# A gated bilinear unit beside an FFT filter: new dependences, priorities and load estimates in a list-scheduled kernel

## The chip, the cores and the metric

The kernel runs on one core of one Trainium2 chip. A core has TensorE (PE, matrix products into PSUM), VectorE (DVE), ScalarE (ACT), GpSimd (POOL), SyncE (SP, which here issues DMAs) and 16 DMA engines. The metric is the device time in microseconds of one execution; for each kernel the median of several is given.

## The reference

The input x has 2048 rows of 640 bf16 values. Each row is normalized, and two things are computed from the normalized rows: a two-dimensional real FFT that is multiplied by a complex weight and transformed back, and a bilinear gated unit. Both are added to x.

```python
def _layernorm(x, axis=-1, eps=1e-5):
    m = jnp.mean(x, axis=axis, keepdims=True)
    v = jnp.var(x, axis=axis, keepdims=True)
    return (x - m) / jnp.sqrt(v + eps)
...
    X = rfft2(x.astype(jnp.float32)); X = X * (w_r + 1j * w_i); y = irfft2(X, s=(S, D)).astype(jnp.bfloat16)
...
    g = jnp.einsum("bsd,df->bsf", x, w_gate)
    u = jnp.einsum("bsd,df->bsf", x, w_up)
    return jnp.einsum("bsf,fd->bsd", g * u, w_down)
...
    xn = _layernorm(x, axis=-1)
    return x + _A_ref(xn, A_w_r, A_w_i) + _B_ref(xn, B_w_gate, B_w_up, B_w_down)
```

(The transforms' lambdas are written out shorter here; S is 2048, D 640, F 1536.)

## The kernel before

**Tiles.** x lies in SBUF as 16 "rows" b = 0 to 15, each a tile of 128 partitions by 640 values (2048 / 16 tokens). It comes in six loads (`_X_LOADS`): rows 0, 1, 2 and 3 each alone, then 4 to 7, then 8 to 15. The gate and up weights come in five pairs of loads (`_GW_LOADS`): of the 12 column blocks f of 128, blocks 0-1, 2-3, 4-5, 6-7, and 8-11. All these go through SP's queue, in one order, except the first up load and a small table, which ACT issues.

**A planner decides the order.** Nothing runs in the order in which the source makes it. `_build` makes tasks (`T`, `dma`), each with an engine or a choice of two, a modelled duration, a priority, and dependences that follow from what it reads and writes (or are added by hand in `deps`). `_Sched.plan` is a list scheduler: for each engine it takes the ready task of best priority, lets another go first that would end within that task's start plus a slack (`slack`, per engine), and thereby fixes one static order per engine, as well as which engine makes a copy and which PSUM bank a product gets. Loads are modelled by bytes over `dma_bw` plus `_DMA_LAT`. The modelled times do nothing on the chip; there each engine walks through its list in that order, and waits at each task for the semaphores of its dependences. So an instruction that waits holds all that stand behind it on its engine.

**Normalizing a row** (lines 758 to 821). For rows 0 to 5: two statistics instructions on DVE (`bn`, L778), their merge (`ag`, L786), adding epsilon (`ve`, L799), a square root on ACT (`sd`, L803), a reciprocal on DVE (`rs`, L807), and two passes over the row: subtract the mean (`sub`, L814) and scale (`mul`, L821, tasks `muls[b]`). For rows 6 to 15 the statistics are made on ACT: `sm` (L763, the mean) and `sq` (L769, the squares), each an ACTIVATE that accumulates, followed by a read of the accumulator, and merged on DVE (`mb`, L791). From row 4 on, two rows share `ve`, `sd` and `rs`.

**Transposing.** Rows 0 to 3 are transposed by PE: `T0_b`, five products with the identity (L839) into PSUM, copied to the tile XT by ACT and DVE in two parts for rows 0 and 1, in one part for rows 2 and 3 (L715 on ACT, L716 on DVE). Rows 4 to 15 go by a transposing DMA that SP issues when the row is scaled (`xt`, L827).

**Gate and up products.** `GU_f_b` multiplies XT of a chunk of rows by the weight block f; the chunks are rows 0; 1; 2-3; 4-7; 8-11; 12-15. For the first two chunks one task holds ten matmuls of 128 columns, for rows 2-3 ten of 256 (both L984), from row 4 on gate and up are two tasks of five matmuls with 512 columns (L964). Such a task holds one PSUM bank, and at most two may be held by this class (cap "glu"); a copy to SBUF frees it (`eG`, nearly always ACT, L715: 128 x 256 for the first chunks, 128 x 512 after them), and DVE multiplies the two (`H`, L1001 and L1000) into the tile HT.

**The transform.** Steps `S1` to `S5` on DVE (L878 to L912) combine pairs of normalized rows, `R` (L925, five matmuls for each row, copied out by `eR`) begins the transform along the rows, `D` (L1029), `C` (L1050 to L1053), the product with the complex weight (`WM`, L1065 to L1068) and `IA` (L1112, L1113) follow, then `I` (L1141) and `V1` to `V5` on DVE.

**The end.** For each row a and half, `ACC` (L1216) sums twelve matmuls of 320 columns from HT and the down weights, `IV` (L1224) adds the last product of the transform into the same bank, DVE adds x (`FIN`, L1231), and SP stores the result.

**At the start.** PE runs 48 matmuls on zeros (L743) and then, while it has nothing to do, pairs of filler products (L732, L733).

The units of gate and up products are put in order by when their rows (`c_at`) and weights (`w_at`) are due:

```python
        w_at = [6.0 + opts.get("w_rate", 2.2) * min(ft // 2, 4) for ft in range(12)]
        c_at = [6.3 + opts.get("c_rate", 2.2) * (b0 + nb - 1) for b0, nb in _CHUNKS]
```

and by hand row 1's statistics are held back, the first until row 0 is scaled and the second until its transposed copy is made:

```python
                    if b == 1:
                        bns[0].deps.add(muls[0])
                        bns[1].deps.add(e0_first)
```

Of the kernel before, what the change touches and what calls it, by code (L numbers as in the profile page):

```python
# [12 lines left out]
_TAIL = {"pe": 165.0, "act": 90.0, "dve": 90.0, "pool": 100.0, "sp": 0.0}  # L13
_DMA_BW = 350.0
_DMA_LEAD = 500.0
_DMA_LAT = 1000.0
_START = 680.0
_DMA_ISSUE = 500.0

# [52 lines left out]
class _Sched(object):  # L72
    def __init__(self):
        self.tasks = []
        self.bufs = []
        self.caps = {}
        self.window = 250.0
        self.affinity = 600.0
        self.dma_bw = _DMA_BW
        self.slack = {"pe": 1000.0, "act": 300.0, "dve": 400.0, "pool": 100.0, "sp": 0.0}  # L80
        self.order = None
        self.makespan = 0.0

    def buf(self, name, off, size):
# [69 lines left out]
    def plan(self, nbanks=8, filler_deadline=0.0):  # L154
# [56 lines left out]
        while nsch < ntot:  # L211
# [41 lines left out]
            for e_ in by_eng:  # L253
                lst = by_eng[e_]
                hb = None
                for c in lst:
                    k = (c[3].prio, c[0], c[3].tid)
                    if hb is None or k < hb[0]:
                        hb = (k, c)
                hc = hb[1]  # L260
                slack = self.slack.get(e_, 100.0)
                ch_ = None
                for c in lst:
                    if c is hc or c[1] <= hc[0] + slack:
                        k = (c[0], c[3].prio, c[3].tid)
                        if ch_ is None or k < ch_[0]:
                            ch_ = (k, c)
                c = ch_[1]
                k = (c[0], c[3].prio, c[3].tid)
                if pick is None or k < pick[0]:  # L270
                    pick = (k, c)
            est, fin, e, t, unit_choice = pick[1]
# [26 lines left out]
            if unit_choice is not None:  # L299
                k0 = unit_choice[1]  # L300
                nb = 2 if unit_choice[0] == "pair" else 1
# [247 lines left out]
def _build(nc, A_x, A_w_r, A_w_i, B_w_gate, B_w_up, B_w_down, out, opts=None):  # L549
# [3 lines left out]
    with es:  # L553
# [153 lines left out]
        def dma(name, dst, src, nbytes, writes, prio, semkey=None, reads=(), after=(), q="sp"):  # L707
            def em(c):
                return c.e.dma_start(dst, src)  # L709
            return T(name, q, _DMA_ISSUE, em, reads=reads, writes=writes, prio=prio, nbytes=nbytes,  # L710
                     semkey=semkey, after=after)
# [40 lines left out]


        for gi, (b0, nb) in enumerate(_X_LOADS):
            dma("ld_x%d" % gi, v_x[:, b0:b0 + nb, :], xv[:, b0:b0 + nb, :], 128 * nb * 1280,
                [(b_x, ("s", b0, b0 + nb))], prio=(0.0, 0.003, 0.02, 0.03, 0.042, 0.06)[gi])
        muls = {}
        for gi, (b0, nb) in enumerate(_LN_GROUPS):
            pbase = 1.0 + 0.05 * gi if gi < 4 else opts.get("ln_prio", 5.9) + 0.05 * (gi - opts.get("ln_lead", 2))
            for b in range(b0, b0 + nb):  # L760
                if b >= opts.get("act_stats", 6):
                    def em_sm(c, b=b):
                        return c.e.activation(v_jk, v_x[:, b, :], _ACTF.Copy, scale=1.0 / _D,  # L763
                                              accum_out=v_m32[:, b:b + 1])
                    T("sm%d" % b, "act", _d_act(640) + 93, em_sm, reads=[(b_x, ("s", b, b + 1))],
                      writes=[(b_m32, ("b", b, b + 1)), (b_jk, None)], prio=pbase)

                    def em_sq(c, b=b):
                        return c.e.activation(v_jk, v_x[:, b, :], _ACTF.Square, scale=-1.0, bias=v_m32[:, b:b + 1],  # L769
                                              accum_out=v_ss[:, b:b + 1])  # L770
                    T("sq%d" % b, "act", _d_act(640) + 186, em_sq,
                      reads=[(b_x, ("s", b, b + 1)), (b_m32, ("b", b, b + 1))],
                      writes=[(b_ss, ("b", b, b + 1)), (b_jk, None)], prio=pbase)
                else:
                    bns = []
                    for i in range(2):
                        def em_bn(c, b=b, i=i):
                            return c.e.bn_stats(v_st[:, b, 6 * i:6 * i + 6], v_x[:, b, 320 * i:320 * i + 320])  # L778
                        bns.append(T("bn%d_%d" % (b, i), "dve", 420.0, em_bn, reads=[(b_x, ("s", b, b + 1))],
                                     writes=[(b_st, ("b", 2 * b + i, 2 * b + i + 1))], prio=pbase))  # L780
                    if b == 1:
                        bns[0].deps.add(muls[0])
                        bns[1].deps.add(e0_first)

                    def em_ag(c, b=b):
                        return c.e.bn_aggr(v_mv[:, b, :], v_st[:, b, :])  # L786
                    T("ag%d" % b, "dve", 176.0, em_ag, reads=[(b_st, ("b", 2 * b, 2 * b + 2))],
                      writes=[(b_mv, ("b", b, b + 1))], prio=pbase)
# [151 lines left out]
        for i, (f0, nf) in enumerate(_GW_LOADS):  # L940
            for w_ in range(2):
                dma("ld_gw%d_%d" % (f0, w_), v_gw[:, w_, :, f0:f0 + nf, :].rearrange("p j r f -> p j (r f)"),
                    gvs[w_][:, :, f0 * 128:(f0 + nf) * 128], 5 * 128 * nf * 256,
                    [(b_gw, ("s", w_ * _NGW + f0, w_ * _NGW + f0 + nf))], prio=(0.004, 0.012, 0.022, 0.032, 0.05)[i] + 0.001 * w_,
                    q="act" if w_ and i < 1 else "sp")
        w_at = [6.0 + opts.get("w_rate", 2.2) * min(ft // 2, 4) for ft in range(12)]
        c_at = [6.3 + opts.get("c_rate", 2.2) * (b0 + nb - 1) for b0, nb in _CHUNKS]
        units = sorted((max(c_at[ci], w_at[ft | 1]), ci, ft) for ci in range(len(_CHUNKS))
                       for ft in range(0, 12, 1 if _CHUNKS[ci][1] == 4 else 2))
        for ui, (at_, ci, ft0) in enumerate(units):  # L950
# [177 lines left out]
            dma("ld_wd%d" % f0, v_wd[:, f0:f1], wdv[:, f0:f1], 128 * (f1 - f0) * 1280,  # L1128
                [(b_wd, ("e", 640 * f0, 640 * f1))], prio=18.0 if f0 < 7 else 9.6, after=[muls[opts.get("w_after", 15)]])
        for a in range(16):  # L1130
            pa = 19.0 + opts.get("i_rate", 0.05) * a
            pc = 41.0 + 0.05 * a
            r2 = a % 2

# [68 lines left out]
        for a in range(16):  # L1203
            pc = opts.get("acc_prio", 41.0) + 0.05 * a
            xs = a % 4
            dma("ld_xr%d" % a, v_xr[:, xs, :], xv[:, a, :], 128 * 1280, [(b_xr, ("r", xs, xs + 1))],
                prio=pc, semkey=("xr", xs))
            for hf in range(2):
                ro = 2 * (a % 2) + hf
                sl3 = slice(hf * 320, (hf + 1) * 320)  # L1210

                def em_ag2(c, a=a, sl3=sl3):
                    bk = bank_of(c.t)
                    ins = None
                    for ft in _FT_ORDER:
                        ins = c.e.matmul(ps[:, bk, 0:320], v_ht[:, ft, a * 128:(a + 1) * 128], v_wd[:, ft, sl3],  # L1216
                                         start=(ft == 7), stop=False)
                    return ins
                ag2 = T("ACC_%d_%d" % (a, hf), "pe", 12 * _d_mm(320), em_ag2,
                        reads=[(b_ht, ("col", a, a + 1)), (b_wd, None)],  # L1220
                        prio=pc + 0.01 + 0.001 * hf, bank="single", cls="acc")

                def em_iv(c, ag2=ag2, a=a, sl3=sl3):
                    return c.e.matmul(ps[:, bank_of(ag2), 0:320], v_sm[:, 2, :], v_v[:, a, sl3], start=False,  # L1224
                                      stop=True)
                iv = T("IV_%d_%d" % (a, hf), "pe", _d_mm(320), em_iv,
                       reads=[(b_v, ("a", a, a + 1)), (b_sm, ("t", 1, 3))], prio=opts.get("iv_prio", 19.0) + 0.05 * a + 0.01 + 0.001 * hf, after=[ag2])

                def em_f1(c, ag2=ag2, a=a, xs=xs, sl3=sl3):
                    bk = bank_of(ag2)  # L1230
                    return c.e.tensor_tensor(v_out[:, a % 2, sl3], ps[:, bk, 0:320], v_xr[:, xs, sl3], _OP.add)  # L1231
                f1 = T("FIN_%d_%d" % (a, hf), "dve", _d_dve_psum(320), em_f1,
                       reads=[(b_xr, ("r", xs, xs + 1))], writes=[(b_out, ("r", ro, ro + 1))], prio=opts.get("fin_prio", 41.0) + 0.05 * a - 0.001,
                       frees=ag2, after=[iv])
                dma("st_out%d_%d" % (a, hf), ov[:, a, sl3], v_out[:, a % 2, sl3], 128 * 640, [], prio=pc - 0.003,
                    reads=[(b_out, ("r", ro, ro + 1))], semkey=("out", ro))

        sch.window = 100.0
        sch.slack["act"] = opts.get("slack_act", 500.0)
        sch.slack["dve"] = opts.get("slack_dve", 600.0)  # L1240
        sch.slack["pe"] = opts.get("slack_pe", 1500.0)
        sch.affinity = opts.get("affinity", 300.0)
        sch.dma_bw = float(opts.get("dma_bw", 310.0))
        sch.plan(8, filler_deadline=opts.get("fill_deadline", 7600.0))
        sch.compute_waits()
        if opts.get("report") is not None:
# [75 lines left out]
```

## Time and profile before

| | |
|---|---|
| median of 4 executions | 208.67 us (207.82, 208.33, 209.01, 209.74) |
| the profiled execution | 207.82 us, its span in the profile 206.0 us |
| granted TensorE clock | 1.000 |
| HBM read, written | 16.82 MB, 2.62 MB |

The span is what the profile sees, from the first to the last instruction; the execution's time is 1.82 us longer. The page's coarse view of the span, 40 slices of 5.15 us, each digit the busy share in tenths:

```profile
PE   7988999999999999999999999999999999999994
DVE  4698999999999999949997996917999999999941
ACT  2377989999876666577999899878422022000000
DMA  6999990603118843001323353225033133224211
```

TensorE's row is full but for the first 20 us and the end; the DMA engines are full from about 5 to 30 us, while the weights, the rows and the tables come in. "PE" in the views is the matmuls, "PEld" the weight loads that overlap them. In the timelines an instruction's entry has its start, its duration, engine, line and operation, and in brackets how long its engine was idle before it and what ended that.

### The profile page before, as it was taken

What the parts mean: (1) busy time and instruction counts of PE and PEld (TensorE: products, weight loads), DVE (VectorE), ACT (ScalarE), POOL (GpSimd) and SP (SyncE); (2) the same over time, 40 slices, a digit from 0 to 9 for tenths busy, and PEclk for the clock granted to TensorE, in tenths of its full rate; (3) what the DMA queues carried; (4) which work ended last, traced back from release to release, by engine and by line L of the source; (5) the groups of instructions that cost most, each with busy time, mean ns of one, the idle gap of its engine ahead of it and who ended that gap; (6) DMA issues with size and microseconds to landing.
All of it is one profiled execution on the core that took longest, in us unless ns stands there. A gap on an engine that the chain in (4) does not pass through costs nothing.

```text
span 206.0 us, 4482 instructions
## 1 busy us (share of the span) xinstructions
PE 200.7 (97%) x1682; PEld 136.5 (66%) x1682; DVE 178.2 (87%) x507; ACT 121.3 (59%) x282; POOL 21.8 (11%) x36
## 2 busy tenths in 40 slices
PE   7988999999999999999999999999999999999994
PEld 7888899645455455465766666656777777777772
DVE  4698999999999999949997996917999999999941
ACT  2377989999876666577999899878422022000000
POOL 0000000000000000003655365310000000000000
PEclk9999999999999999999999999999999999999999
DMA  6999990603118843001323353225033133224211
GB/s 182 300 342 378 393 198 7 61 6 64 32 33 73 251 111 122 3 0 24 68 58 61 62 119 67 67 65 158 3 98 93 44 104 121 86 67 112 83 48 48
DMA packets 30596, 21.69 MB, mean 105 GB/s; under 512 B 10480, under 2 KB 29552, under 8 KB 30448
## 3 DMA queue, kind: packets, MB, share of 16 engines
q1 hardware_dynamic: 29776, 21.06, 41.2%
q10 hardware_dynamic: 800, 0.36, 0.6%
q8 instruction: 13, 0.21, 0.5%
q14 instruction: 7, 0.06, 0.1%
HBM read 16.82 MB, written 2.62 MB: 94 GB/s over the span
## 4 chain that ended last, share of the span: by engine, by line
PE 89%; SPq 4%; DMA 4%; DVE 1%; issue 0%; DVEq 0%
PE ps L964 38%; PE ps L1216 25%; PE ps L984 9%; SPq L709 4%; DMA arena<-in_A_x_dram 4%; PE ps L1029 2%; PE ps L1113 2%; PE ps L925 2%; PE ps L1141 2%; PE ps L1112 2%; PE ps L1224 2%; PE ps L1050 1%; PE ps L1053 1%; PE ps L1052 1%; PE ps L1051 1%; DVE arena L778 1%
## 5 line engine op out<-in xcount | busy, mean ns | idle before, releaser
L715 ACT ACTIVATE arena<-ps 128x512 bf16<-128x512 f32 (+6 forms) x182 | 96.7, 567 | 48.7 <-PE ps L1141 22.6
L964 PE MATMUL ps<-arena 128*128 128x512 bf16 x360 | 82.6, 379 | 0.0
L964 PEld LDWEIGHTS ps<-arena 128*128 128x128 bf16 x360 | 33.8, 98 | 36.5 <-ACT arena L715 1.4
L1216 PE MATMUL ps<-arena 128*128 128x320 bf16 x384 | 56.5, 299 | 0.0
L1216 PEld LDWEIGHTS ps<-arena 128*128 128x128 bf16 x384 | 37.3, 98 | 14.1
L984 PE MATMUL ps<-arena 128*128 128x128 bf16 (+1 forms) x360 | 27.9, 237 | 1.3 <-DVE arena L799 0.6
L984 PEld LDWEIGHTS ps<-arena 128*128 128x128 bf16 x360 | 25.2, 98 | 3.4 <-ACT arena L715 1.4
L1065 DVE TENSOR_TENSOR arena<-ps,arena 128x256 f32<-128x256 f32 x64 | 22.6, 417 | 1.4 <-PE ps L1053 1.4
L1000 DVE TENSOR_TENSOR arena<-arena 128x512 bf16<-128x512 bf16 x36 | 15.4, 427 | 8.8 <-ACT arena L715 8.7
L1088 POOL TENSOR_TENSOR arena<-arena 128x256 bf16<-128x256 f32 x16 | 10.4, 647 | 112.9 <-DVE arena L1081 112.9
L1231 DVE TENSOR_TENSOR arena<-ps,arena 128x320 bf16<-128x320 f32 x32 | 15.6, 486 | 5.0 <-PE ps L1224 4.9
L1089 POOL TENSOR_TENSOR arena<-arena 128x256 bf16<-128x256 f32 x16 | 11.9, 745 | 0.0
L1112 PE MATMUL ps<-arena 128*128 128x128 bf16 x80 | 10.4, 219 | 0.0
L1113 PE MATMUL ps<-arena 128*128 128x128 bf16 x80 | 10.4, 219 | 0.0
L1112 PEld LDWEIGHTS ps<-arena 128*128 128x128 bf16 x80 | 8.7, 111 | 1.7
L1113 PEld LDWEIGHTS ps<-arena 128*128 128x128 bf16 x80 | 8.7, 112 | 1.4
L1224 PE MATMUL ps<-arena 128*128 128x320 bf16 x32 | 9.1, 299 | 0.0
L878 DVE TENSOR_TENSOR arena<-arena 128x384 f32<-128x384 bf16 x16 | 8.8, 552 | 0.0
L778 DVE BATCH_NORM_STATS2 arena<-arena 128x6 f32<-128x320 bf16 x12 | 5.6, 484 | 3.8 <-DMA arena<-in_A_x_dram 3.6
L769 ACT ACTIVATE arena<-arena 128x640 bf16<-128x640 bf16 x10 | 8.3, 827 | 0.0
L763 ACT ACTIVATE arena<-arena 128x640 bf16<-128x640 bf16 x10 | 7.3, 729 | 0.8 <-DMA arena<-in_A_x_dram 0.8
L1001 DVE TENSOR_TENSOR arena<-arena 128x256 bf16<-128x256 bf16 (+1 forms) x18 | 6.0, 331 | 1.5 <-ACT arena L715 1.5
(73 smaller groups left out, 237.9 us busy)
## 6 DMA issues: line engine op xcount, KB each, us to landing
arena<-in_A_x_dram SPq DMA_DIRECT2D x20, 160.0 KB, 2.4
out_dram<-arena SPq DMA_DIRECT2D x32, 80.0 KB, 1.6
arena<-c_tf SPq DMA_DIRECT2D x4, 384.0 KB, 10.9
arena<-in_A_w_r_dram SPq DMA_DIRECT2D x32, 40.1 KB, 2.3
arena<-in_A_w_i_dram SPq DMA_DIRECT2D x32, 40.1 KB, 2.3
arena<-in_B_w_gate_dram SPq DMA_DIRECT2D x4, 320.0 KB, 5.5
arena<-in_A_x_dram SPq DMA_DIRECT2D x1, 1280.0 KB, 9.9
arena<-c_ti SPq DMA_DIRECT2D x2, 512.0 KB, 4.9
```

Source lines behind the costliest of these rows:

```text
L715: return c.e.activation(dst, src, _ACTF.Copy)
L964: ins = c.e.matmul(ps[:, bk, :], v_gw[:, w, j, ft, :], v_xt[:, j, rows], start=(j == 0), stop=(j == 4))
L984: ins = c.e.matmul(ps[:, bk, w * n:(w + 1) * n], v_gw[:, w, j, ft, :], v_xt[:, j, rows], start=(j == 0), stop=(j == 4))
L1000: return c.e.tensor_tensor(v_ht[:, ft0, rows], v_gbf[:, rr, 0, :], v_gbf[:, rr, 1, :], _OP.mult)
L1065: c.e.tensor_tensor(v_p[:, ar, w, :, 128 * h:128 * h + 128].rearrange("p c (m k) -> p c m k", k=4), xh.rearrange("p c (m k) -> p c m k", k ...
L1088: c.e.tensor_tensor(v_y[ar][:, 512:768], p01[:, 0:256], p10[:, 0:256], _OP.add)
L1089: return c.e.tensor_tensor(v_y[ar][:, 256:512], p00[:, 0:256], p11[:, 0:256], _OP.subtract)
L1112: c.e.matmul(dst, l1, v_ti[:, t, 0, :], start=True, stop=False)
L1113: ins = c.e.matmul(dst, l2, v_ti[:, t, 1, :], start=False, stop=True)
L1216: ins = c.e.matmul(ps[:, bk, 0:320], v_ht[:, ft, a * 128:(a + 1) * 128], v_wd[:, ft, sl3], start=(ft == 7), stop=False)
L1224: return c.e.matmul(ps[:, bank_of(ag2), 0:320], v_sm[:, 2, :], v_v[:, a, sl3], start=False, stop=True)
L1231: return c.e.tensor_tensor(v_out[:, a % 2, sl3], ps[:, bk, 0:320], v_xr[:, xs, sl3], _OP.add)
```

## The change

Four kinds of edit, all in what the planner is told; the instructions themselves and the number of them that a task makes stay the same.

- Dependences: the first statistics instruction of rows 2 and 3 now also waits for the scaling of the row ahead, as that of row 1 did.
- Urgency: a task named in `urgent` (the four `T0`), when it is the best of its engine, lets another go first only if that ends within 100 ns of its start, instead of PE's slack of 1500.
- Load estimates: latency 1150 for 1000, bandwidth 380 for 310, and more bytes for some loads (an x row alone 1400 for 1280 per partition, the load of four rows 1800; weights of two blocks 340 for 256, of four blocks 280).
- Priorities: `ln_prio` and `ln_lead` (rows 4 and on), `c_rate` (when rows are due for the gate and up products), `i_rate`, `iv_prio`, `fin_prio` (the end).

```diff
-_DMA_LAT = 1000.0
+_DMA_LAT = 1150.0
...
+        self.urgent = ()
...
                 slack = self.slack.get(e_, 100.0)
+                if hc[3].name in self.urgent:
+                    slack = 100.0
...
-            dma("ld_x%d" % gi, v_x[:, b0:b0 + nb, :], xv[:, b0:b0 + nb, :], 128 * nb * 1280,
+            dma("ld_x%d" % gi, v_x[:, b0:b0 + nb, :], xv[:, b0:b0 + nb, :], 128 * nb * (1800 if nb == 4 else 1400 if nb == 1 else 1280),
...
-            pbase = 1.0 + 0.05 * gi if gi < 4 else opts.get("ln_prio", 5.9) + 0.05 * (gi - opts.get("ln_lead", 2))
+            pbase = 1.0 + 0.05 * gi if gi < 4 else opts.get("ln_prio", 5.99) + 0.05 * (gi - opts.get("ln_lead", 4))
...
+                    if 1 <= b <= 3:
+                        bns[0].deps.add(muls[b - 1])
                     if b == 1:
-                        bns[0].deps.add(muls[0])
                         bns[1].deps.add(e0_first)
...
-                    gvs[w_][:, :, f0 * 128:(f0 + nf) * 128], 5 * 128 * nf * 256,
+                    gvs[w_][:, :, f0 * 128:(f0 + nf) * 128], 5 * 128 * nf * (340 if nf == 2 else 280),
...
-        c_at = [6.3 + opts.get("c_rate", 2.2) * (b0 + nb - 1) for b0, nb in _CHUNKS]
+        c_at = [6.3 + opts.get("c_rate", 1.8) * (b0 + nb - 1) for b0, nb in _CHUNKS]
...
-            pa = 19.0 + opts.get("i_rate", 0.05) * a
+            pa = 19.0 + opts.get("i_rate", 0.2) * a
...
                iv = T("IV_%d_%d" % (a, hf), "pe", _d_mm(320), em_iv,
-                       reads=[(b_v, ("a", a, a + 1)), (b_sm, ("t", 1, 3))], prio=opts.get("iv_prio", 19.0) + 0.05 * a + 0.01 + 0.001 * hf, after=[ag2])
+                       reads=[(b_v, ("a", a, a + 1)), (b_sm, ("t", 1, 3))], prio=opts.get("iv_prio", 30.0) + 0.05 * a + 0.01 + 0.001 * hf, after=[ag2])
...
                f1 = T("FIN_%d_%d" % (a, hf), "dve", _d_dve_psum(320), em_f1,
-                       reads=[(b_xr, ("r", xs, xs + 1))], writes=[(b_out, ("r", ro, ro + 1))], prio=opts.get("fin_prio", 41.0) + 0.05 * a - 0.001,
+                       reads=[(b_xr, ("r", xs, xs + 1))], writes=[(b_out, ("r", ro, ro + 1))], prio=opts.get("fin_prio", 5.0) + 0.05 * a - 0.001,
...
+        sch.urgent = opts.get("urgent", ('T0_0', 'T0_1', 'T0_2', 'T0_3'))
...
-        sch.dma_bw = float(opts.get("dma_bw", 310.0))
+        sch.dma_bw = float(opts.get("dma_bw", 380.0))
```

What the planner makes of it, task by task, in the first 30 us (`U4` stands for the four units `GU_6_0`, `GU_7_0`, `GU_6_1`, `GU_7_1`):

```
PE before: T0_0 fillers GU_0_0 GU_1_0 GU_2_0 GU_3_0 T0_1 GU_0_1 GU_1_1 GU_2_1 T0_2 GU_3_1 GU_4_0 GU_5_0 GU_4_1 GU_5_1 T0_3 U4 GU_0_2 .. GU_6_2 R_0 R_1 GU_7_2 GU_8_0
PE after:  T0_0 fillers GU_0_0 GU_1_0 GU_2_0 T0_1 GU_3_0 GU_0_1 GU_1_1 T0_2 GU_2_1 GU_3_1 GU_4_0 GU_5_0 T0_3 GU_4_1 GU_5_1 GU_0_2 .. GU_5_2 U4 GU_6_2 GU_7_2 GU_8_0 R_0 R_1
DVE before, from the reciprocal of row 1: rs1 bn2 mul1 bn2 H ag2 copy(T0_1) ve2 sub2 H rs2 bn3 mul2 bn3 H ag3 ve3 sub3 S1_0 rs3 H mul3 H bn4 ..
DVE after:                                rs1 mul1 bn2 bn2 copy(T0_1) ag2 H ve2 sub2 H rs2 mul2 bn3 bn3 H ag3 ve3 sub3 rs3 mul3 H S1_0 H bn4 ..
ACT before, from the copies of GU_4_0: eG eG eG sm6 copy(T0_3) eG eG eG eG eG sq6 sd eG sm7 eG sq7 eG eG sm8 ..
ACT after:                             eG eG copy(T0_3) eG eG sm6 eG sq6 eG sm7 eG sd eG sq7 eG sd eG eG sm8 ..
```

The order of the loads on SP is the same in both. Later in the program `R_2` to `R_7` stand one to three units earlier on PE, `xt6` and `xt7` follow `xt5` directly on SP, `xt12` comes behind `S2_3` to `S5_3`, three copies go from DVE to ACT (`eR_0`, `eR_3`, `eR_5`) and three tasks from ACT to DVE (`eR_6`, one copy of `GU_3_4`, `mul15`), some `ACC` go ahead of an `IV`, and `FIN` goes ahead of steps of `V` on DVE.

## The prediction

> **What bounds the kernel now.** I read the page first, for who is full.
>
> ```profile
> PE 200.7 (97%) x1682; PEld 136.5 (66%) x1682; DVE 178.2 (87%) x507; ACT 121.3 (59%) x282; POOL 21.8 (11%) x36
> PE 89%; SPq 4%; DMA 4%; DVE 1%; issue 0%; DVEq 0%
> ```
>
> TensorE is the chain: 89% of it. The matmul count stays the same (7 filler pairs too), so only its 5.3 us of idle can be won. The windows say where that lies (columns: PE, weight loads, DVE, ACT, POOL busy; clock; DMA share; GB/s):
>
> ```profile
> 0.00:6.10 6.10, 5.05 (x49) 5.05 (x50) 2.78 (x10) 1.49 (x2) 0.21 (x4) 1.00 0.72 200
> 6.10:19.36 13.26, 11.87 (x197) 10.90 (x195) 10.89 (x40) 8.46 (x25) 0.00 (x0) 1.00 1.14 338
> 19.36:30.00 10.64, 10.64 (x114) 9.73 (x115) 10.22 (x33) 9.73 (x24) 0.00 (x0) 1.00 1.14 316
> 30.00:60.00 30.00, 30.00 (x225) 17.96 (x223) 28.75 (x91) 27.05 (x65) 0.00 (x0) 1.00 0.33 41
> 90.00:140.00 50.00, 49.84 (x439) 32.36 (x438) 39.54 (x130) 43.94 (x118) 21.59 (x32) 1.00 0.30 65
> ```
>
> From 19.36 to the last matmul PE is full. The change can only pull that full stretch forward, or tear holes in it. So the time is decided before about 26 us, and the timeline there has the waits:
>
> ```profile
> 9.20 0.49 DVE L778 BATCH_NORM_STATS2 arena<-arena 128x6 f32<-128x320 bf16 x1 [0.57 <-DMA arena<-in_A_x_dram]
> 9.62 0.37 DVE L821 TENSOR_SCALAR arena<-arena 128x640 bf16<-128x640 bf16 x1
> 10.04 0.45 PE L839 MATMUL ps<-arena 128*128 128x128 bf16 x5
> ...
> 16.21 0.44 PE L839 MATMUL ps<-arena 128*128 128x128 bf16 x5
> 16.48 2.40 PE L984 MATMUL ps<-arena 128*128 128x128 bf16 x40
> 16.79 0.74 ACT L763 ACTIVATE arena<-arena 128x640 bf16<-128x640 bf16 x1 [0.85 <-DMA arena<-in_A_x_dram]
> ...
> 17.52 2.06 ACT L715 ACTIVATE arena<-ps 128x640 bf16<-128x640 bf16 x6
> ...
> 19.36 0.66 PEld L984 LDWEIGHTS ps<-arena 128*128 128x128 bf16 x7 [0.65 <-ACT arena L715]
> ```
>
> Row 1's scaling (L821) stands behind row 2's statistics, which wait for row 2's load until 9.20. And on ACT the copy of T0_3 and four GU copies (the x6 at 17.52) stand behind sm6 (L763), which waits for rows 4 to 7 (landing 9.20 + 7.6 = 16.8); PE, done with GU_7_1 at 18.16 + 0.56 = 18.72, waits 0.64 for the last of them.
>
> **The change, stepped through.** The order is the one in which each engine's instructions stand in the changed program. All loads up to the tables keep their issue order, so I keep their landings (issue plus time to landing): up weights 2-3 at 8.69, row 2 at 9.18, up weights 4-5 at 11.40, row 3 at 11.90, rows 4-7 at 16.77. The new bytes, bandwidth and latency move nothing on the queue; they only reorder.
>
> *Row 1.* The reciprocal starts at 8.47 as before; scaling follows 0.20 later (L807 4.79, L821 4.99) and takes 0.36: done 9.03. PE is then in GU_2_0, held by its weights to 8.78, plus ten matmuls at 0.056: T0_1 at 9.34, not 10.04. DVE: statistics of row 2 at 9.20 and 9.61, T0_1's copy at 10.03, done 10.33. PE: T0_1 0.28, GU_3_0 0.56, free at 10.18; with 0.14 from copy to matmul (10.92 to 11.06) GU_0_1 starts at 10.47, not 11.06.
>
> *Row 2.* From that copy the rows' start-to-start steps are 0.22 and 0.12 (ag, H), 0.20, 0.06, 0.29 (ve, sub, H), 0.20, 0.20 (rs, mul), then 0.37: done 11.69, T0_2 at 11.74 against 12.85. PE, free at 10.47 + 20 x 0.056 = 11.59, waits 0.15.
>
> *Row 3.* Statistics start at its landing, 11.92; 0.41 + 0.41 + 0.20 + 0.24 + 0.07 + 0.37 + 0.20 brings the scaling to 13.82, done 14.19 (S1_0, 1.69 us, now stands behind it). PE does T0_2 and GU_2_1 to GU_5_0 (2.24) until 14.26: T0_3 at once, against 16.21. GU_4_1 and GU_5_1 end at 15.66; T0_3's copy on ACT (0.69 from 14.75) is done at 15.44, no longer behind sm6. So the same matmuls that end at 16.48 now end at 15.66: 0.82 won.
>
> *What comes next differs.* Before: four units GU_6/GU_7 (2.24), the 0.64 wait, six units of 256 columns (1.095 each), GU_6_2 at 25.92. After: the six first, the four behind them. Each of the six needs one of two PSUM banks, freed by an ACT copy of 0.59, and the changed order puts sm6, sq6, sm7, sq7 between those copies. sm6 16.79 to 17.52; copy to 18.11; GU_2_2 at 18.16 where PE is free at 15.66 + 2.19 = 17.85: wait 0.31. sq6 from 18.0 (0.87), copy 18.87 to 19.46: GU_3_2 at 19.51, where PE is free at 19.26: wait 0.25. sm7 (0.73 from 19.35), copy 20.08 to 20.67: GU_4_2 at 20.72, wait 0.11. Then PE is slower than ACT again. GU_6_2 starts at 15.66 + 6.57 + 0.67 + 2.24 = 25.14: 0.78 earlier. The 0.64 wait is all but replaced by 0.67; what is won is the row chains.
>
> *Beyond 25 us.* Rows 6 and 7 are scaled right behind row 5, so their two transposing DMAs leave SP behind xt5 (24.6) instead of at 27.5, into loads that still land until 28.6; GU_0_4_0 needs them near 37.4, and before the later landed at 32.9: free, with 4 us of cover. mul12 and its DMA now stand behind S2_3 to S5_3, up to 4 us later, for products near 96. R_2, R_4, R_6 are called one to three units (1.08 each) earlier. R_2 goes ahead of GU_11_2 and GU_0_4_0, its place becomes 38.67 - 2.17 - 0.78 = 35.7; its input S5_1 ended at 37.75, and ahead of it on DVE now go eR_0 (0.82, to ACT), a reciprocal, a scaling and an H: 1.78 less 4 overlaps of 0.08 is 1.46, so 36.3 at worst, 35.2 if the 1.1 us that DVE idles between 19.36 and 37.75 (8.72 of 9.14, 8.58 of 9.25) goes too. Cost 0 to 0.6; I take 0.1, nearer to the idle, which waits on copies that come earlier now. eR_0 on ACT costs 0.70 in a stretch with 2.95 idle of 30. At the end some ACC go ahead of an IV (ACC_14_1 of IV_14_0) and FIN ahead of V: PE's order is permuted at equal length, IV_14_0 gets 1.63 later on PE against 0.4 more DVE work (FIN_13_1) ahead of V5_14. I take 0: nothing can be gained, as PE was full and the tail after the last matmul is the same; FINs that wait ahead of V could cost up to 0.3.
>
> Sum: -0.78 + 0.1 = -0.7 on a span of 206.0, whose execution took 207.82 (1.82 outside the span, kept); the median of the four runs is 208.67, so **208.0**.
>
> New waits of PE on banks could touch its clock. The granted clock is 1.00 from 6.10 to 19.36, with waits up to 0.74 (10.04 + 0.28 to 11.06) and the last of 0.64 on a bank, so nothing is charged. [...]
>
> **Rivals.**
>
> *More is won.* ACT keeps up, the 0.67 is not paid: 208.67 - 1.4 = 207.3. For: the order between copies could slip in PE's favour. Against: ACT is strictly in order at 16.79 and its rows leave no room: 0.59 + 0.8 against 1.095 of PE.
>
> *Nothing is won.* The three waits become 1.4: each statistics pass 0.25 longer between copies. For: each is followed by a read of its accumulator (0.19 to 0.24) of which I count a part. Against: 17.43 + 0.19 overlaps the next start at 17.52. Then 208.7.
>
> *Slower: R comes before its input.* If S1 to S5 move up by nothing on DVE, R_2 at 35.7 waits for 37.75 and R_4 (47.86 - 3.24 - 0.78 = 43.8) for 47.25: 3.4 in all, since the first wait delays the second. -0.78 + 3.4: 211.3. It decides from S5_2's end: past 44.6 the gain is gone. For: DVE is busy 28.75 of 30. Against: 2.9 us of work (eR_0, eR_3, two subs, two Hs and small ones) leaves the queue ahead of S5_2.
>
> **Numbers.** Forecast 0.67, more won 0.11, nothing 0.12, slower 0.10. Run to run the kernel before spreads from 207.82 to 209.74, so 1% (2.1 us) is about what can be told from no change. Range 206.9 to 209.7: low is 207.3 less a further 0.4 of small PE waits, high takes the nothing case, the costs 0.6 and 0.3 and the lower part of the slower case; outside lie its upper part and run spread. Faster by over 1% (below 206.6) needs the whole of the first rival and more: 0.06. Slower by over 1% (above 210.8) is the upper half of the slower case, and 0.01 for run spread: 0.06. Within: 0.88.
>
> **What would show it.** T0_1, T0_2, T0_3 near 9.3, 11.7, 14.3; GU_0_2 near 15.7; three waits of PE on ACT between 17.8 and 20.8, 0.67 together; the first 512-column matmul near 37.4 (37.59 - 0.78, plus 0.56 of R_2 and R_3 ahead of it); PE full after that, R_2 with no wait over 0.3; the last matmul near 202.6 instead of 203.3. It would be wrong if a load landed elsewhere than before, if ACT waits exceeded 1.4, or if a window after 30 us showed PE short by a microsecond.

## The result and the profile after

| | before | after |
|---|---|---|
| median | 208.23 us (79 executions, 207.25 to 209.77) | 207.55 us (53 executions, 206.71 to 208.44) |
| ratio | | 0.9963, 95% interval 0.9954 to 0.9971 |
| profiled execution, its span | 207.82, 206.0 us | 207.47, 205.6 us |
| T0_1, T0_2, T0_3 start | 10.04, 12.85, 16.21 | 9.35, 11.70, 14.22 |
| GU_0_2, GU_6_2 start | 19.36, 25.92 | 15.62, 24.92 |
| last matmul ends | 203.33 | 202.95 |

The change is worth 0.37%, some 0.7 us, which is less than the spread of single executions and shows only in the medians of many. The median of the kernel before is 208.23 when 79 executions are taken, not the 208.67 of the first four, from which the prediction came to its 208.0; what it forecast is the difference, 0.7 us.

The page's engine totals and its chain of waits, after:

```profile
PE 200.9 (98%) x1682; PEld 136.0 (66%) x1682; DVE 179.2 (87%) x507; ACT 121.4 (59%) x282; POOL 21.8 (11%) x36
PE 86%; DMA 5%; SPq 4%; DVE 3%; issue 1%; ACT 0%; DVEq 0%
```

The work is the same: 1682 matmuls, 200.9 us of them. Of the DMA share of 5% in the chain, 2% is a load of the filter's weights (in_A_w_i) late in the program, for which PE waits; it comes up again below. The windows (columns as before):

```profile
6.10:19.36 13.26, 12.77 (x188) 11.47 (x185) 11.43 (x42) 9.44 (x26) 0.00 (x0) 1.00 1.14 337
19.36:30.00 10.64, 10.64 (x140) 9.59 (x139) 10.42 (x34) 10.21 (x27) 0.00 (x0) 1.00 1.13 318
30.00:60.00 30.00, 30.00 (x215) 17.55 (x213) 29.26 (x92) 27.14 (x63) 0.00 (x0) 1.00 0.29 40
90.00:140.00 50.00, 49.52 (x429) 31.91 (x428) 39.79 (x129) 43.63 (x117) 21.57 (x32) 1.00 0.32 68
```

From 6.10 to 19.36 us PE is busy 12.77 us instead of 11.87: 0.9 us won there. From 90 to 140 us it is busy 49.52 instead of 49.84: 0.3 lost again, in a stretch that the change does not seem to touch. The timeline after shows how the first part was won:

```profile
8.64 0.39 DVE L825 TENSOR_SCALAR arena<-arena 128x640 bf16<-128x640 bf16 x1
9.18 0.89 DVE L781 BATCH_NORM_STATS2 arena<-arena 128x6 f32<-128x320 bf16 x2 [0.15 <-DMA arena<-in_A_x_dram]
9.35 0.44 PE L843 MATMUL ps<-arena 128*128 128x128 bf16 x5
...
14.22 0.44 PE L843 MATMUL ps<-arena 128*128 128x128 bf16 x5
14.42 1.78 ACT L718 ACTIVATE arena<-ps 128x256 bf16<-128x256 f32 x4 [0.17 <-PE ps L988]
14.50 6.23 PE L988 MATMUL ps<-arena 128*128 128x128 bf16 x61
...
16.58 0.74 ACT L766 ACTIVATE arena<-arena 128x640 bf16<-128x640 bf16 x1 [0.38 <-DMA arena<-in_A_x_dram]
...
17.95 0.99 PEld L988 LDWEIGHTS ps<-arena 128*128 128x128 bf16 x10 [0.26 <-ACT arena L718]
...
19.24 0.99 PEld L988 LDWEIGHTS ps<-arena 128*128 128x128 bf16 x10 [0.31 <-ACT arena L718]
```

Row 1's scaling (L825) is over when row 2's load lands at 9.18, where it used to wait for it. T0_3 runs at 14.22, and its copy is among the four that ACT makes from 14.42, ahead of sm6 (L766), which waits for rows 4 to 7 until 16.58. PE's line at 14.50 holds 61 matmuls in a row. Then the weight loads of GU_2_2 and GU_3_2 wait 0.26 and 0.31 for ACT's copies, at 17.95 and 19.24: those are the waits that the prediction put there.

### The profile page after: what moved, and what is told of

It reads as the page before. It is cut to its first block, busy times and chain, and to the rows that moved or that the text cites. A ratio compares the mean times of both kernels' runs of the same rounds, so it can differ in the third digit from the quotient of the medians.

```text
span 205.6 us, 4485 instructions
## 1 busy us (share of the span) xinstructions
PE 200.9 (98%) x1682; PEld 136.0 (66%) x1682; DVE 179.2 (87%) x507; ACT 121.4 (59%) x282; POOL 21.8 (11%) x36
## 4 chain that ended last, share of the span: by engine, by line
PE 86%; DMA 5%; SPq 4%; DVE 3%; issue 1%; ACT 0%; DVEq 0%
PE ps L968 34%; PE ps L1220 25%; PE ps L988 12%; SPq L712 4%; DMA arena<-in_A_x_dram 3%; PE ps L1145 2%; PE ps L929 2%; PE ps L1228 2%; DMA arena<-in_A_w_i_dram 2%; PE ps L1033 1%; PE ps L1116 1%; PE ps L1117 1%; DVE arena L1069 1%; PE ps L1054 1%; PE ps L1057 1%; PE ps L1055 1%
## 5 line engine op out<-in xcount | busy, mean ns | idle before, releaser
L718 ACT ACTIVATE arena<-ps 128x512 bf16<-128x512 f32 (+5 forms) x183 | 97.0, 568 | 48.5 <-PE ps L1145 22.8
L1220 PE MATMUL ps<-arena 128*128 128x320 bf16 x384 | 55.9, 299 | 0.0
L1220 PEld LDWEIGHTS ps<-arena 128*128 128x128 bf16 x384 | 37.4, 98 | 14.2
L988 PE MATMUL ps<-arena 128*128 128x128 bf16 (+1 forms) x360 | 28.5, 237 | 0.5 <-DMA arena<-in_B_w_up_dram 0.3
L1235 DVE TENSOR_TENSOR arena<-ps,arena 128x320 bf16<-128x320 f32 x32 | 14.9, 486 | 4.2 <-PE ps L1228 4.1
L1228 PE MATMUL ps<-arena 128*128 128x320 bf16 x32 | 8.3, 299 | 0.0
L766 ACT ACTIVATE arena<-arena 128x640 bf16<-128x640 bf16 x10 | 7.3, 734 | 0.5 <-DMA arena<-in_A_x_dram 0.4
L1072 DVE TENSOR_TENSOR arena<-ps,arena 128x260 f32<-128x260 f32 x16 | 7.0, 438 | 0.0
```

Source lines behind the costliest of these rows:

```text
L718: return c.e.activation(dst, src, _ACTF.Copy)
L988: ins = c.e.matmul(ps[:, bk, w * n:(w + 1) * n], v_gw[:, w, j, ft, :], v_xt[:, j, rows], start=(j == 0), stop=(j == 4))
```

## The experiments

Twelve kernels ran. Edits marked "order" move a task in its engine's list after the planner is done; everything else is planned anew. Times are medians; a ratio is to the kernel before, run on the same chip beside it, with its 95% interval (it is not the plain quotient of the two medians).

### e1: the row chains alone

```diff
 order of DVE, kernel before:
+mul1 ahead of the first bn of row 2, mul2 ahead of the first bn of row 3, S1_0 behind H_4
```

> The kernel before with its planned order, except on DVE: the scaling of rows 1 and 2 goes ahead of the statistics of rows 2 and 3, and S1_0 goes behind the scaling of row 3. PE's and ACT's orders stay as before. Theory A (the prediction's words: what is won is the row chains): T0_1, T0_2, T0_3 come near 9.9, 12.5, 15.7 instead of 10.04, 12.85, 16.21, and the end comes about 0.5 us earlier, ratio 0.9975. Theory B (a gate: GU_0_2 waits for copies that stand on ACT behind sm6, and sm6 for the landing of rows 4 to 7 at 16.8): the transposes come as early, but GU_0_2 still starts at 19.36, its wait grows from 0.64 to about 1.15, and the time is that of before, ratio 1.000 within 0.001.

Measured: 208.23 against 208.55, ratio 0.9981 (0.9957 to 1.0005). The timeline:

```profile
15.79 0.44 PE L870 MATMUL ps<-arena 128*128 128x128 bf16 x5
...
16.79 0.74 ACT L794 ACTIVATE arena<-arena 128x640 bf16<-128x640 bf16 x1 [1.06 <-DMA arena<-in_A_x_dram]
...
19.36 0.83 PE L1015 MATMUL ps<-arena 128*128 128x256 bf16 x6 [0.89 <-ACT arena L746]
```

T0_3 comes 0.42 earlier than before (15.79 against 16.21), and GU_0_2 starts at 19.36, where it started before; only its wait on ACT has grown. GU_6_2 is at 25.92, as before. In this profile the row chains by themselves win nothing by 25 us: T0_3's copy still stands on ACT behind sm6, sm6 behind a load that lands at 16.8. The times alone do not tell the two theories apart, since the interval holds both 0.9975 and 1.000.

### e2 and e3: the load estimates alone, and everything but them

```diff
 e2, kernel before (e3 takes the same lines out of the kernel after):
-_DMA_LAT = 1000.0
+_DMA_LAT = 1150.0
...
+ bytes of the loads (x rows 1800, 1400 for 1280; weights 340, 280 for 256)
-        sch.dma_bw = float(opts.get("dma_bw", 310.0))
+        sch.dma_bw = float(opts.get("dma_bw", 380.0))
```

> The kernel before with the planner's load estimates of the change alone (latency, bandwidth, bytes); no new dependence, no urgency, old priorities. In its order row 1's scaling stands ahead of row 2's statistics all the same, and on ACT the copy of T0_3 and three GU copies stand ahead of sm6. Theory A with the dependences as the cause: at most a part of the gain, T0_3 comes at 15.8 and not at 14.2, so 0.4 us, ratio 0.998. Theory C (the estimates make the order, and the order past sm6 makes the time): no wait at GU_0_2, the whole gain of the change, ratio 0.996.

> The changed kernel with the old load estimates; dependences, urgency and all priorities stay changed. Theory A: dependences and urgency carry the row chains, so most of the gain stays, ratio 0.997. Theory C: the gain goes, ratio 1.000 within 0.001, T0_1 at 10.0 again, since the planner puts the other half of row 2's statistics ahead of row 1's scaling.

Measured: e2 207.89, ratio 0.9964 (0.9938 to 0.9990); e3 208.71, ratio 1.0001 (0.9979 to 1.0023). By the medians the estimates alone have the whole gain, and the change without them has none. Timeline of e2:

```profile
16.03 1.87 ACT L715 ACTIVATE arena<-ps 128x256 bf16<-128x256 f32 x4 [0.18 <-PE ps L984]
16.14 3.92 PEld L984 LDWEIGHTS ps<-arena 128*128 128x128 bf16 x56
16.20 4.03 PE L984 MATMUL ps<-arena 128*128 128x128 bf16 x55
...
17.80 0.73 ACT L763 ACTIVATE arena<-arena 128x640 bf16<-128x640 bf16 x1
```

With loads of four rows modelled as later, the planner puts sm6 behind the copies instead of ahead of them: ACT copies from 16.03, sm6 starts at 17.80, and its entry names no wait for the load. PE runs 55 matmuls from 16.20 without a gap, although T0_3 is at 15.91, only 0.3 earlier than before. Its lists also have the row chains of e1: rows 1 and 2 are scaled ahead of the next row's statistics (T0_1 at 9.92, T0_2 at 12.10). So e2 has both, the row chains and the copies ahead of sm6. GU_6_2 starts at 25.62, with R_0 and R_1 (0.56 together) now ahead of it, so like for like at 25.06. (e2's profiled execution is the second quickest of its twelve.)

e3 has only one of the two. ACT's list has the copy of T0_3 ahead of sm6 there as well, without the estimates; it is among these four copies:

```profile
15.49 1.79 ACT L718 ACTIVATE arena<-ps 128x256 bf16<-128x256 f32 x4 [0.17 <-PE ps L988]
17.60 0.74 ACT L766 ACTIVATE arena<-arena 128x640 bf16<-128x640 bf16 x1 [0.33 <-DMA arena<-in_A_x_dram]
```

What e3 lacks is the row chains: row 1's scaling stands behind one half of row 2's statistics, which waits for its load until 9.58, and T0_1, T0_2 and T0_3 come at 10.42, 13.32 and 15.29. GU_6_2 is at 26.31; the loads landed 0.4 to 0.8 later in this execution than before (sm6 at 17.60), so that number by itself says little, and the 12 executions carry the verdict. So copies ahead of sm6 win nothing without the row chains, as the row chains win nothing by 25 us without them (e1). e3's lists differ from those of the change later on too, so this is no test of the chains alone, and which of the other edits puts the copy ahead of sm6 in e3 was not run.

### e4: the new dependences alone

```diff
+                    if 1 <= b <= 3:
+                        bns[0].deps.add(muls[b - 1])
                     if b == 1:
-                        bns[0].deps.add(muls[0])
                         bns[1].deps.add(e0_first)
```

> The kernel before with the new dependences alone. Theory A: rows 1 and 2 are scaled earlier, 0.3 to 0.5 us won, ratio 0.998. Theory C: nothing won, since the dependence holds one half of a row's statistics and the order has the other half there, waiting for the same load; T0_1 at 10.0, T0_2 at 12.9, ratio 1.000 to 1.0015.

Measured: 208.69, ratio 0.9996 (0.9975 to 1.0017): nothing. DVE's timeline of e4 shows why the named edit does so little:

```profile
9.13 0.49 DVE L778 BATCH_NORM_STATS2 arena<-arena 128x6 f32<-128x320 bf16 x1 [0.37 <-DMA arena<-in_A_x_dram]
9.54 0.37 DVE L822 TENSOR_SCALAR arena<-arena 128x640 bf16<-128x640 bf16 x1
9.83 0.29 DVE L1002 TENSOR_TENSOR arena<-arena 128x256 bf16<-128x256 bf16 x1
10.03 0.49 DVE L778 BATCH_NORM_STATS2 arena<-arena 128x6 f32<-128x320 bf16 x1
```

The dependence binds the first of row 2's two statistics instructions. The planner puts the second one, which is free of it, ahead of row 1's scaling (L822), and it waits for the same load, 0.37 us. In the kernel after, the dependence changes nothing either: without its lines for rows 2 and 3 the planner gives the same lists, but for which half of the statistics comes first (planned, not run).

### e5: the change without its three end priorities

```diff
-i_rate 0.2, iv_prio 30.0, fin_prio 5.0
+i_rate 0.05, iv_prio 19.0, fin_prio 41.0
```

> The changed kernel with the old priorities of the end (i_rate, iv_prio, fin_prio); the order up to the first ACC stays that of the change. Theory (prediction: the end is a permutation of a full PE and costs or wins nothing): the time of the changed kernel, ratio to before 0.996. Rival, the end makes the gain: ratio 1.000; rival, FIN ahead of V costs what is won earlier: ratio 0.9945.

Measured: 207.44, ratio 0.9951 (0.9925 to 0.9977). They do not make the gain.

### e6: the gate put back

```diff
 order of ACT, kernel after:
+sm6 ahead of the copy of T0_3
```

> The changed kernel with one task moved: on ACT sm6 goes back ahead of the copy of T0_3, as it was before; everything else in the order of the change, with its earlier transposes. Theory B (the gate): sm6 starts at 16.8 again with rows 4 to 7, the copy at 17.5, GU_0_2 at 18.2 instead of 15.6, a wait of 2.6 on PE, of which the waits behind it (0.45) fall away: about 2.0 us longer than the changed kernel, 1.2 longer than before, ratio 1.006. Theory A (the row chains carry it): the transposes at 9.35, 11.7, 14.2 keep a good part of the gain, ratio below 1.000.

Measured: 210.30 (6 executions, 209.44 to 211.86), ratio 1.0109 (1.0063 to 1.0155). The direction is the theory's, the size is larger than expected. Waits of PE, and the windows around them (seventh number: granted clock):

```profile
PE ps L1019 <- ACT arena L749: 2.6, 1, 2.6
```

```profile
15.80:18.50 2.70, 0.07 (x2) 0.02 (x2) 0.91 (x3) 1.49 (x4) 0.00 (x0) 1.00 1.13 359
18.50:19.50 1.00, 1.00 (x10) 0.90 (x11) 0.50 (x2) 0.47 (x2) 0.00 (x0) 1.00 1.08 398
19.50:23.00 3.50, 3.50 (x20) 2.43 (x18) 2.35 (x10) 2.47 (x5) 0.00 (x0) 0.51 1.00 396
23.00:30.00 7.00, 6.97 (x83) 6.28 (x82) 6.24 (x22) 5.94 (x17) 0.00 (x0) 1.00 1.15 285
```

PE stands still for 2.6 us, works again from 18.48, and a microsecond later its granted clock is 0.51 for 3.5 us: 20 matmuls of 256 columns, where 32 fit at 0.11 us each; 3.5 x 0.49 = 1.7 us of full clock lost on top of the wait. By the mean clock of 0.992 that happened in two of the six executions (211.14 and 211.86 us, the second of them profiled); the four at 1.000 took 209.44 to 210.39, whose middle, 209.86, is 1.006 of 208.61, the ratio expected from the wait alone.

### e7: half as many, larger loads of the filter's weights

This was to test the loss from 90 to 140 us. There the weight of each filter row comes in four loads of 40 KB, and the filter's product C of a row is held until its four have landed. The edit loads the same bytes with two for each row.

```diff
-                for h in range(2):
-                    k2 = int(_rows(t, 0, h, 0))
-                    dma("ld_w%d_%d_%d" % (t, w_, h), v_w[64 * h:64 * h + 64, wr, w_, 0:321], wvs[w_][:, k2, :],
...
+                ka, kb = int(_rows(t, 0, 0, 0)), int(_rows(t, 0, 1, 0))
+                dma("ld_w%d_%d" % (t, w_), v_w[:, wr, w_, 0:321],
+                    wvs[w_][:, ka:kb + 1:kb - ka, :].rearrange("k h l -> h k l"),
...
```

> The changed kernel with the filter's weights loaded by half as many DMAs (one for both halves of the partitions, 32 instead of 64); the order on all compute engines is that of the change. In the changed kernel's profile C_12 and C_15 wait 0.34 and 0.42 for these loads, and SP issues them without a gap, 0.64 each, from 94 to 127 us. If SP's issue time is what they wait for, both waits go: 0.7 us, ratio to before 0.993. Rival, the transfers themselves are late or the waits are chance of that one execution: 0.996 as the change.

Measured: 223.07, ratio 1.0715 (1.0678 to 1.0752): a miss by 15 us. SP's timeline of e7, and the waits of PE from 30 to 140 us:

```profile
98.59 1.81 SPq L712 DMA_DIRECT2D arena<-in_A_w_r_dram  x1
100.44 1.94 SPq L712 DMA_DIRECT2D arena<-in_A_w_i_dram  x1
102.43 2.16 SPq L712 DMA_DIRECT2D arena<-in_A_w_r_dram  x1
```

```profile
PE ps L1054 <- DMA arena<-in_A_w_i_dram: 9.0, 6, 2.7
```

One load of 80 KB in this form keeps SP for some 1.9 us in a long row of them, where two of 40 KB take 1.24 (the same view after, "98.77 1.23 ... x2"). A row of the filter then costs SP 2 x 1.9 = 3.9 us, and the products C follow at that pace (C_10 to C_15 start at 125.92, 129.48, 133.43, 137.31, 141.22 and 145.21; after, they come 2.6 us apart on average). So the test of a remedy failed. Nor does it show that SP's issuing paces PE, for here the transfers are what is slow:

- The first loads after a pause keep SP for only 0.51 us each (at 94.17, 94.72 and 96.25).
- From 100 to 115 us the DMA engines move 42 to 45 GB/s at a mean busy share of 0.14 to 0.15 (after: 56 to 64 at 0.30 to 0.32), and at that rate 80 KB take 1.8 to 2.0 us.
- C_6 starts at 108.94, 8.5 us after its last load was issued at 100.44; a load of 40 KB in the kernel after mostly lands 2.3 us after its issue.

These three fit an SP that, too, waits behind the transfers; what it waits for was not shown by itself. Why this form of load is slow was not tried. Some 1.7 of the 15 us are clock: the window from 120 to 125 us has a granted clock of 0.66 (5 x 0.34), behind a wait of PE of 2.7 us, and all six executions have a mean clock of 0.991 or 0.992.

### e8: rows 4 to 7 loaded ahead of two pairs of up and gate weights

```diff
-                prio=(0.0, 0.003, 0.02, 0.03, 0.042, 0.06)[gi])
+                prio=(0.0, 0.003, 0.02, 0.03, 0.0315, 0.06)[gi])
```

> The changed kernel with the load of rows 4 to 7 issued ahead of the weights 6-7 (which the new order needs only at 22.7); the planner orders anew. Rows 4 to 7 should land near 14 instead of 16.6 and the weights by 17. If that landing is what ACT's passes wait for, the three PE waits between 17.8 and 20.8 (0.45 together) go, GU_6_2 comes near 24.4 instead of 24.9, and the end 0.3 to 0.5 earlier than the change, ratio 0.994. Rival: ACT's own work is the limit (copy 0.59 and pass 0.8 against 1.095 of PE), the waits return somewhat later, ratio 0.996.

Measured: 207.58, ratio 0.9963 (0.9935 to 0.9990): the same as the change. ACT in the timeline:

```profile
14.92 0.74 ACT L766 ACTIVATE arena<-arena 128x640 bf16<-128x640 bf16 x1 [0.66 <-DMA arena<-in_A_x_dram]
...
16.39 4.70 PEld L988 LDWEIGHTS ps<-arena 128*128 128x128 bf16 x44 [0.77 <-ACT arena L718]
```

The rows land 1.7 us earlier, and the planner takes sm6 ahead of the copy of T0_3 again. So it is not the place of sm6 by itself that costs, but the landing for which it waits. The three small waits of the change (0.45) become one of 0.77 at GU_0_2; GU_6_2 is at 25.18 instead of 24.92.

### e9: only the order of the products

```diff
-        c_at = [6.3 + opts.get("c_rate", 2.2) * (b0 + nb - 1) for b0, nb in _CHUNKS]
+        c_at = [6.3 + opts.get("c_rate", 1.8) * (b0 + nb - 1) for b0, nb in _CHUNKS]
```

> The kernel before with one number changed: the products of rows 2 and 3 are due earlier (c_rate 1.8), with the old load estimates. So the six units of 256 columns stand ahead of the four units of GU_6 and GU_7, as in the change, but row 3's statistics stay behind nothing new and row 3's transposed copy on ACT stays behind sm6, which waits for rows 4 to 7 until 16.8. Theory (the order of the products gains only with the copy ahead of sm6): GU_0_2 waits about 1.9 us for that copy, from 16.4 to 18.3 us; GU_6_2 near 27.0 instead of 25.92; the time some 1.1 to 1.3 above before, ratio 1.005 to 1.006, and 1.6 more in an execution whose clock closes as in two of six of the kernel with the copy behind sm6. Rival (moving the six units up is what wins): GU_6_2 near 25.1, ratio 0.996.

Measured: 209.85 (10 executions, 208.41 to 212.20), ratio 1.0070 (1.0043 to 1.0098). The six units ahead of the four, with the copy of T0_3 behind sm6, is a loss, as expected. The profiled execution was the quickest of the ten; in it rows 4 to 7 landed early (sm6 at 15.64) and PE waited 0.8 rather than 1.9. Two of the ten show a mean clock of 0.992, at 211.2 and 212.2 us, as in e6.

### e10: the row chains and the gate together

```diff
 order, kernel before: the three edits of e1 on DVE, and on ACT
+sm6 behind the copy of GU_7_1
```

> The kernel before with the row chains of e1 (scaling of rows 1 and 2 ahead of the next row's first statistics, S1_0 out of row 3's way) and, on ACT, sm6 moved behind the copies of T0_3 and of the gate and up units; the order of PE stays that of before. Theory (the two edits win only together): T0_3 15.7 to 15.8, GU_0_2 at 18.9 with no wait on ACT instead of 19.36, GU_6_2 near 25.5; 0.4 earlier, ratio 0.998, which is two thirds of what the change wins by 25 us at most, since the four units ahead no longer have the six units' room. Rival (the row chains are worth nothing even with ACT free): GU_6_2 25.9, ratio 1.000. Rival (ACT's statistics, now later, hold up rows 6 and 7 or the copies behind them): GU_6_2 26 or later, or new waits of PE on ACT between 19 and 26 us.

Measured: 208.50, ratio 1.0008 (0.9989 to 1.0026). In the profile the theory's steps are there (T0_3 15.68, GU_0_2 18.98, GU_6_2 25.56, 0.36 earlier than before), though PE's weight load still waits 0.77 at GU_0_2 for a copy of ACT, which the theory had at nothing. The gain in time is not there. What took it in this execution, in the waits of PE from 90 to 140 us:

```profile
PE ps L1081 <- DMA arena<-in_A_w_i_dram: 0.5, 1, 0.5
```

C_7 waited there 0.7 for its weights, counted from the end of the work ahead of it, against 0.05 in the kernel before; the last of its loads landed 3.03 us after its issue.

### e11 and e12: one load out of the filter's way, and the end priorities undone as well

```diff
 e11, order of SP, kernel after:
+ld_wd0 behind the last load of the filter's weights
 e12: e11, and i_rate 0.05, iv_prio 19.0, fin_prio 41.0
```

> The changed kernel with one load of down weights (320 KB, issued by SP at 115.9 us, 0.6 us of SP's time) moved behind the last load of the filter's weights. Theory (in the stretch from 94 to 127 us the filter's products C keep step with SP, which takes 0.62 us for each of 48 loads of 40 KB, and so give back part of what was won before): the loads behind it are issued 0.6 earlier, the waits of C_12 (0.34) and C_15 (0.42) shrink to under 0.15 each, PE is busy 49.8 or more of the 50 us from 90 to 140, and the time is 0.3 to 0.6 below the change's: ratio to before 0.993 to 0.995. Rival (those waits are for PSUM banks or for the products ahead of them): both stay within 0.1 of what they are, ratio 0.996.

> The kernel of e11 (the changed kernel with one load of down weights behind the filter's weights) with the three end priorities as before the change (i_rate 0.05, iv_prio 19, fin_prio 41). In the changed kernel and in e11 PE loses 0.10 us at each of two of the transform's last products (I_12 and I_14, near 164 and 172 us), which before does not. Theory (those two waits come from FIN ahead of V on DVE): they are gone, the last matmul is 0.2 us earlier against GU_6_2 than in e11 (202.56 - 24.92 = 177.64 there, so near 177.4), and the ratio to before is 0.994 or a little less. Rival (the end priorities are neutral or help): 177.6 or more, ratio 0.995 or more.

Measured: e11 207.19 (207.07 to 207.60), ratio 0.9948 (0.9929 to 0.9968); e12 207.20, ratio 0.9960 (0.9943 to 0.9976), beside a kernel before that had 208.11 instead of 208.55. The window of e11 from 90 to 140 us:

```profile
90.00:140.00 50.00, 49.93 (x437) 32.25 (x435) 39.84 (x130) 43.99 (x119) 21.58 (x32) 1.00 0.31 70
```

PE is busy 49.93 of 50 us instead of 49.52. C_12 no longer waits and C_15 waits 0.22 instead of 0.42, with 0.18 new at C_9; GU_6_2 is at 24.92 in both, and the last matmul ends at 202.56 instead of 202.95. The profile bears out the theory for C_12: its loads in the kernel after landed 2.3 us after their issue, as most do, so they were issued too late, and here they are early enough. It does not for C_15, whose wait stays above the 0.15 that was allowed. Its cause is in the chain of waits of the kernel after:

```profile
126.03 3.59 DMA arena<-in_A_w_i_dram
...
129.67 0.31 PE ps L1054
```

The last load for C_15, issued at 126.03, took 3.59 us to land. With 2.3 it would have been there at 128.3, and PE was free for C_15 at 129.67 - 0.42 = 129.25. So here a transfer was late, as the rival of e7 had it, and not SP. In e11 the same load took 3.30. Across the profiled executions (e7 apart) it took 2.2 (e2) to 3.7 us (e9); what makes it late was not tried.

The waits of PE's weight loads from 140 to 180 us, first e11, then e12 (L1176 is the product I):

```profile
PEld ps L1176 <- issue: 0.5, 2, 0.2
PEld ps L1176 <- DVE arena L1210: 0.2, 1, 0.2
```

```profile
PEld ps L1176 <- DVE arena L1210: 0.2, 1, 0.2
```

The two waits of I are gone with the old priorities, as they are in e5. (PE itself loses less by them, 0.10 each, since it is still at the product before: in the kernel after I_12 starts 0.24 behind the IV ahead of it, where in the kernel before it starts 0.14 behind it.) In e12 the last matmul ends 177.03 after GU_6_2 starts, against 177.64 in e11: 0.2 of that was expected from I_12 and I_14, the rest are the waits of C, of which e12's execution has none. By the times e11 and e12 are best of all, 207.2, but their intervals overlap that of the change, and e12 is not told apart from e11.

## Why the prediction was right, point by point

The table has the stations of those profiled executions whose matmul records are complete (start of GU_6_2, end of the last matmul); "idle" is PE's from 90 to 140 us, 50 less its busy time in the window.

| | execution | GU_6_2 | idle | last matmul ends |
|---|---|---|---|---|
| before | 207.82 | 25.92 | 0.16 | 203.33 |
| after | 207.47 | 24.92 | 0.48 | 202.95 |
| e1 row chains | 208.61 | 25.92 | 0.77 | 204.12 |
| e2 estimates | 206.95 | 25.06 (like for like) | 0.07 | 202.45 |
| e3 no estimates | 208.91 | 26.31 | 0.03 | 204.39 |
| e4 dependences | 209.25 | 26.03 | 0.78 | 204.74 |
| e9 order alone | 208.41 | 26.04 | 0.29 | 203.91 |
| e10 chains and gate | 208.22 | 25.56 | 0.64 | 203.71 |
| e11 load moved | 207.07 | 24.92 | 0.07 | 202.56 |

**The steps up to 25 us held.** T0_1 9.35 (9.34 forecast), T0_2 11.70 (11.74), T0_3 14.22 (14.26), GU_0_2 15.62 (15.66), the first 512-column matmul 37.27 (37.4). The three waits on ACT came where they were put, at GU_2_2, GU_3_2 and GU_4_2, but with 0.14, 0.20 and 0.11 they make 0.45, not 0.67: rows 4 to 7 landed 0.2 earlier, so sm6 began at 16.58 instead of 16.79. That is the whole of the 0.2 by which GU_6_2 is earlier than forecast.

**The reason given was incomplete.** "The 0.64 wait is all but replaced by 0.67; what is won is the row chains" is true of the sum and not of the cause. e1 has the row chains and wins nothing by 25 us, because the wait on ACT grows by what the rows win. e3 has the copy of T0_3 ahead of sm6 without the row chains, and its time is that of before. e9 has the order of the products and loses. e6 has all but the place of one instruction on ACT, and loses 2.3 us and more. e2 and the change have both, and win. So the win needs both, early rows and a copy of T0_3 that is not held long behind sm6 (in e8 it stands behind sm6, but the load comes early). That these two are enough is not shown: set by hand in the order of before (e10) they win 0.36 by 25 us in the profile, and nothing in the times. The prediction had both in its steps ("no longer behind sm6"), but named one of them as the cause. Of the edits, the load estimates are what brings the two together (e2, e3); the new dependences are evaded by the planner when they stand alone (e4) and, by its lists, change nothing in the whole.

**"PE full after that" failed.** PE is full in every window from 20.6 to 90 us, but in the filter's stretch it loses 0.48 instead of 0.16. There is little to spare in that stretch: the loads of the filter's last twelve rows are issued from 93.78 to 127 us, when the rows' buffers come free, 0.62 us apiece, so 2.5 us for a row's four, with a load of 0.59 and two stalls of 0.8 in between, and the C of after come 38.57 / 15 = 2.57 apart. The prediction took PE for full there before the change; not quite, since C_12 waited 0.28 and C_7 0.05. In the kernel after C_12 waits 0.34 and C_15 0.42, so 0.42 of the 1.0 is lost again.

It is not shown that the early arrival itself brings this loss. The loads move up with PE: the first of the twelve rows' is issued at 94.78 before and at 93.78 after. C_12's wait is nearly the same in both, and C_15's is one load that took 3.59 us to land instead of 2.93. Nor does the loss go with the arrival in the table: before, e1 and e4 have GU_6_2 at 25.92 to 26.03 and idle for 0.16, 0.77 and 0.78; e2 and e11 have it at 25.06 and 24.92, about as early as after, and idle for 0.07. What sets the loss in each execution was not found.

**The end.** It was taken at 0, with up to 0.3 for FIN ahead of V. I_12 and I_14 wait 0.10 each in after and in e11, not before and not in e12, which has the old priorities. So the three end priorities cost 0.2 in the profile. Which of them, and what the products wait for, the profile does not name ("issue"); that it is FIN was only argued.

**The rest held.** R_2 started at 35.62 without a wait (0.1 was charged); rivals "nothing is won" and "R before its input" have no trace. The granted clock was 1.00 in every window from 17.2 to 24 us, through the waits of 0.14, 0.20 and 0.11 us on banks, so to charge nothing for it was right here. The longer waits of e6 and e7 (2.6 and 2.7 us) did go with a lower mean clock (0.992 in both profiled executions).

The sum in the profile is -1.00 + 0.42 + 0.20 = -0.38 (203.33 to 202.95), against -0.7 forecast; the medians differ by 0.68. Two errors of opposite sign, 0.2 more won and 0.6 given back, lie within what single executions differ by, so the agreement of the median with the forecast is partly luck: e11 and e2 show that a profile without the losses stands at 207.0.

## What to carry to other kernels

Where engines run fixed lists, ask of each early wait what stands behind the waiting instruction: here one ACTIVATE that waits for a load kept a shorter chain on another engine from being worth anything by 25 us (e1), and the open place on ACT was worth nothing without the shorter chain (e3). In this case new load times for the planner were worth more than hand-made dependences, which it evades through the next free instruction. And a gain at the start still has to pass the later stages: in the kernel after the weights of the filter's rows 9 to 13 land 0.05 to 0.28 us before their product starts, so a load that lands late by a microsecond takes a part of the gain back.

## What the runs showed of the hardware

In the profiled execution of e6 an idle stretch of TensorE of 2.6 us was followed by a granted clock of 0.51 for 3.5 us, beginning a microsecond after work had resumed. By their mean clock of 0.992 that happened in two of its six executions; the other four show 1.000. In e7, where the longest wait of PE was 2.7 us and the window from 120 to 125 us has a granted clock of 0.66, all six executions show a mean clock of 0.991 or 0.992. What makes the clock fall, and why it fell in two executions of e6 and not in the other four, was not shown.

A load of 80 KB over 128 partitions, whose source is two rows of the weight rearranged in one access pattern, kept SP for 1.7 to 2.3 us in a long row of its kind and for 0.51 at the start of one, at 42 to 45 GB/s, against 0.6 for each of the two loads of 40 KB over 64 partitions that it replaced, at 56 to 64 GB/s. Fewer and larger DMAs were the slower ones here (ratio 1.0715).
